# Prefix sums in two halves, unread matrix products, and key transposes ahead of the previous chunk's scores, in an attention and mixing kernel

## The chip, the core and the metric

One core of one Trainium2 chip runs the whole program. Its engines are TensorE (PE in the profile, with PEld for its weight loads), VectorE (DVE), ScalarE (ACT), GpSimd (POOL), and SyncE (SP), which here only issues transfers. The metric is device time in microseconds (us), the median of several executions.

## What is computed

The reference runs three layers on 4 batches of 768 steps, with 8 heads of 48 (384 channels).

1. A linear attention with a complex decay. At step t the state of a head decays by a complex number per row, the product of key and value is added, and the output is the query times the real part of the state:

```python
mag = np.sqrt(a_re * a_re + a_im * a_im)
scale = np.minimum(mag, 0.999) / (mag + 1e-06)
for t in range(S):
    new_re = ar * S_re - ai * S_im
    new_im = ar * S_im + ai * S_re
    S_re, S_im = (new_re + k_t v_t, new_im)
    y[t] = q_t @ S_re
```

2. A mixer: `u = x + (relu(x.T @ w_tok1) @ w_tok2).T`, then `u + relu(u @ w_ch1) @ w_ch2`.
3. A gated layer: `xk` and `xr` mix each step with the step before it; the result is `sigmoid(xr @ w_r) * (relu(xk @ w_k)**2 @ w_v)`.

## The kernel before, in words

**Attention of one batch** works on 6 chunks of 128 steps. The logarithm of the decay's magnitude and its angle are summed over time; then each query and key is turned and scaled by its sum, so that within a chunk the output is a masked product of scores with values, and across chunks a state is carried.

The setup stages have letters in the tables `SEQ0` (batch 0) and `SEQ1`: S, L, A and R make log magnitude (`X3`) and angle (`X2`) of three chunks at a time; C J sums chunk J; D makes the scale factors. A sum is a product with a triangular matrix (`tri32`) into one PSUM bank for the magnitude and one for the angle. ScalarE and VectorE take the sum out of the bank; then a product with the complementary triangle (`anti32`) completes the bank's total of the chunk, and the next chunk's triangle is added to it. So each chunk's products wait until the chunk before has been taken out (`sums`, `add`). Batches 0 and 1 do this in fp32, batches 2 and 3 with fp16 halves.

The chunk stages are in `ORD0` and `ORD1`: b turns the angles into cosine and sine (tile `cs`, line 453) and scales (line 458); w splits the value into fp16 high and low parts; q and k rotate (line 473) and take the high part (line 474); e takes the low parts (line 484); u is the state's products, v its evacuation; f0, f1 are the scores of four heads each (`sp`, line 497); m masks them (line 530) and splits off the fp16 high part (line 531); g takes the low part (line 535); h is the output's products (`y`, lines 548 and 550); i takes the output out (`xh`, `xl`, lines 559 and 560). The digit behind a stage says how many steps late it runs, so the stages of neighbouring chunks interleave in the table's order.

Queries and keys of a chunk are turned by DMA transposes, four to a chunk: high and low parts of q and k (line 441). They land in the tile `Rc`. Queries have two places, for odd and even chunks. Keys have two in batch 0 (the second is `kt`), but a single one in batches 1 to 3, so there the next chunk's keys can be transposed only when this chunk's scores have been computed.

**The dense layers** follow, in fp16 halves with three products for one. In batch 0 the first of them is accumulated chunk by chunk during the attention, in two PSUM banks `h1a` and `h1b` (line 598); their evacuation (line 627) starts the rest. The **weights** arrive in 51 pieces of 64-bit words; VectorE rebuilds fp32 from them (lines 258 to 260), ScalarE and VectorE split them into halves (lines 270 and 274), and their range is checked: a sum of squares on ScalarE (line 265), and a smallest value on VectorE (line 267, first 10 pieces) or a second pass on ScalarE (line 269, the others).

**The order.** The batches' attention and dense stages and the weight pieces are generators that are stepped by their estimated costs; the tile scheduler then places every instruction on its engine by priority (`P_EV`, `P_PE`, `P_W`; a larger offset goes earlier) and by data. Each engine runs its instructions in that fixed order. SP issues all transfers, in one fixed order too, and a transfer that must wait holds those behind it.

## Time and profile before

| | us |
|---|---|
| three runs, median | 858.17 |
| their range | 849.31 to 862.32 |
| the profiled execution | 854.39 |
| its span in the profile | 852.6 |
| the first attention (to the first dense evacuation) | 137 |

The profiled execution is one more run, 3.8 us below the median. Engines work side by side, so their busy times do not add up to the span. The trace gives each instruction's start and busy time, what its engine waited for, and the clock that TensorE was granted.

### The profile page before, as it was taken

To read this page: it belongs to the slowest core of one execution; us is meant where nothing else is said; L and a number is where in the kernel's file an instruction comes from. 1 tells how busy PE (TensorE), PEld (TensorE's weight loads), DVE (VectorE), ACT (ScalarE), POOL (GpSimd) and SP (SyncE) were. 2 spreads that over 40 slices of the span, in tenths; PEclk is the share of its full clock that TensorE was granted. 3 is DMA by queue.
4 is the path that set the end of the run, shared out by engine and by line. 5 is a ranking of instruction groups with operands and counts; after the bars stand their busy time and mean duration, and the time that the engine had idled before them with its cause. 6 is when DMAs were issued, how large, how long until landed. Compare 5 with 4: busy or idle time off the path is not lost.

```text
span 852.6 us, 14967 instructions
## 1 busy us (share of the span) xinstructions
PE 736.3 (86%) x5868; PEld 456.2 (54%) x5868; DVE 586.4 (69%) x1152; ACT 557.8 (65%) x1166; POOL 19.5 (2%) x51
## 2 busy tenths in 40 slices
PE   0636758999879978998999899999899999999996
PEld 0214544555545545555565555666565666666563
DVE  5987788999987985976767656776957434151622
ACT  7864559988789868964656769774648543142642
POOL 3000000000000000000000000000000000010000
PEclk9965658999999999999999999999999999999998
DMA  6428793445494394115230850031612420000000
GB/s 204 122 81 164 183 224 124 131 123 162 101 183 121 71 193 100 38 56 130 45 74 15 159 120 23 23 95 41 106 38 60 78 53 2 1 1 1 1 28 32
DMA packets 132941, 74.78 MB, mean 88 GB/s; under 512 B 104576, under 2 KB 126336, under 8 KB 132864
## 3 DMA queue, kind: packets, MB, share of 16 engines
q1 hardware_dynamic: 132864, 73.76, 36.3%
q8 instruction: 48, 0.79, 0.4%
q14 instruction: 29, 0.24, 0.1%
HBM read 43.85 MB, written 4.72 MB: 57 GB/s over the span
## 4 chain that ended last, share of the span: by engine, by line
PE 45%; ACT 20%; DVE 16%; DMA 14%; issue 3%; SPq 0%; ACTq 0%; DVEq 0%
PE ps L598 21%; PE a L598 15%; PE sp L497 3%; ACT X L303 3%; DMA Rc<-ql 3%; DMA Rc<-kl 2%; DMA Rc<-kh 2%; DMA X<-by_time_a_re_dram 2%; DMA CH<-in_qk_dram 2%; ACT tmp L730 1%; PE y L550 1%; ACT ps L765 1%; DMA wst<-in_moe_w_k_dram 1%; DMA wst<-in_moe_w_ch_dram 1%; ACT Rc L531 1%
## 5 line engine op out<-in xcount | busy, mean ns | idle before, releaser
L598 PEld LDWEIGHTS <-wc 128*128 128x128 f16 x1728 | 167.7, 98 | 114.1 <-issue 9.5
L598 PE MATMUL a<-g,wc 128*128 128x384 f16 x864 | 163.9, 327 | 0.0
L598 PE MATMUL ps<-uh,wc 128*128 128x384 f16 x576 | 158.1, 328 | 4.8 <-DVE g L691 3.0
L598 PE MATMUL a<-wv,g 128*128 128x384 f16 x576 | 110.7, 327 | 2.6 <-ACT g L767 2.3
L598 PE MATMUL ps<-xkh,wk 128*128 128x384 f16 x384 | 104.9, 326 | 0.5 <-DVE g L768 0.4
L690 ACT ACTIVATE g<-ps 128x384 f16<-128x384 f32 x96 | 46.5, 484 | 87.0 <-PE ps L598 86.6
L691 DVE SCALAR_TENSOR_TENSOR g<-ps,g 128x384 f16<-128x384 f32 x96 | 53.0, 553 | 73.0 <-ACT g L690 72.8
L598 PE MATMUL ps<-ul,wc 128*128 128x384 f16 x288 | 94.4, 328 | 0.0
L497 PE MATMUL sp<-Rc 96*128 96x128 f16 x504 | 62.5, 235 | 26.7 <-DMA Rc<-kh 16.2
L598 PEld LDWEIGHTS <-g 128*128 128x128 f16 x576 | 54.7, 98 | 38.0 <-ACT g L767 4.5
L598 PEld LDWEIGHTS <-wk 128*128 128x128 f16 x576 | 54.5, 97 | 33.1 <-issue 1.2
L768 DVE TENSOR_TENSOR g<-ps,g 128x384 f16<-128x384 f32 x64 | 35.4, 554 | 47.8 <-ACT g L767 47.5
L598 PE MATMUL ps<-xkl,wk 128*128 128x384 f16 x192 | 62.7, 326 | 0.0
L497 PEld LDWEIGHTS <-Rc 96*128 96x128 f16 x504 | 39.5, 105 | 35.3 <-DMA Rc<-kh 18.6
L765 ACT ACTIVATE ps<-ps 128x384 f32<-128x384 f32 x64 | 30.2, 473 | 39.6 <-PE ps L598 35.4
L548 PE MATMUL y<-CH,Rc 96*128 96x48 f16 x480 | 46.3, 191 | 8.3 <-DMA Rc<-qh 8.2
L515 PE MATMUL u<-CH,kh 128*128 128x48 f16 x320 | 39.1, 193 | 13.5 <-ACT kh L474 13.5
L550 PE MATMUL y<-CH,Rc 128*128 128x48 f16 x504 | 46.4, 190 | 4.8 <-ACT Rc L531 3.6
L473 DVE TENSOR_TENSOR Wc<-cs,X 128x768 f32<-128x768 f32 x48 | 44.9, 951 | 1.5 <-ACT cs L303 1.2
L530 DVE TENSOR_TENSOR m<-sp,tri 128x512 f32<-128x512 f32 x48 | 32.7, 684 | 17.9 <-PE sp L497 17.8
L550 PEld LDWEIGHTS <-Rc 128*128 128x128 f16 x504 | 32.3, 100 | 18.8 <-ACT Rc L531 12.1
L548 PEld LDWEIGHTS <-Rc 96*128 96x128 f16 x480 | 31.9, 102 | 16.7 <-DMA Rc<-qh 11.4
(219 smaller groups left out, 1518.7 us busy)
## 6 DMA issues: line engine op xcount, KB each, us to landing
CH<-in_qk_dram SPq DMA_DIRECT2D x24, 384.0 KB, 3.1
wst<-in_moe_w_ch_dram SPq DMA_DIRECT2D x24, 384.0 KB, 3.3
X<-by_time_a_re_dram SPq DMA_DIRECT2D x8, 576.0 KB, 4.5
X<-by_time_a_im_dram SPq DMA_DIRECT2D x8, 576.0 KB, 5.8
CH<-by_time_v_dram SPq DMA_DIRECT2D x24, 192.0 KB, 2.5
out_dram<-tmp SPq DMA_DIRECT2D x24, 192.0 KB, 1.9
wst<-in_moe_w_tok_dram SPq DMA_DIRECT2D x8, 384.0 KB, 3.4
wst<-in_moe_w_k_dram SPq DMA_DIRECT2D x8, 384.0 KB, 3.6
```

What stands on the lines that cost most here:

```text
L303: ins = ACT(out, x, fn, **k)
L473: TT(d[nm + "2"], d["cs"], bc2(hd((X3 if nm == "q" else X1)[:, J])), op=MUL)
L497: nc.tensor.matmul(out=sp[:, i], lhsT=Tr[J % 2]["k" + a_][0:96, h], rhs=Tr[J % 2]["q" + b_][0:96, h], start=n_ == 0, stop=n_ == 2)
L515: nc.tensor.matmul(out=U[:, h], lhsT=sets[J % 2]["k" + a_][:, h], rhs=d["v" + b_][:, h], start=J == 0 and h == 0 and n_ == 0, stop=h == H ...
L530: TT(m, st[J]["S", g], tri.unsqueeze(1).to_broadcast([128, 4, 128]), op=MUL)
L548: nc.tensor.matmul(out=y[:, h], lhsT=Tr[J % 2]["q" + a_][0:96, h], rhs=b_[:, h], start=n_ == 0, stop=False)
L550: nc.tensor.matmul(out=y[:, h], lhsT=M16[g][m_][:, h % 4], rhs=d[v_][:, h], start=J == 0 and n_ == 0, stop=n_ == 2)
L598: nc.tensor.matmul(out=ps, lhsT=lh[a_], rhs=rh[b_], start=start and n_ == 0, stop=stop and n_ == 2)
L690: ACT(part[:, 0], ps, ACTF.Relu)
L691: STT(part[:, 1], ps, 0.0, part[:, 0], op0=MAX, op1=SUB)
L765: ACT(ps, ps, ACTF.Relu)
L768: TT(part[:, 1], ps, part[:, 0], op=SUB)
```

## The change

It has six parts.

- **Sums of batch 0** (`products`, `add`). Angles and magnitudes of both halves are made first, and then the sums run in the order 0, 3, 1, 4, 2, 5, each half in its own two banks. The second half starts with products of chunks 0 to 2 with a matrix of equal numbers (`ones32`), so it needs no result of the first.
- **A carry instead of the complement.** From chunk to chunk within a half, and in batch 1 from each chunk to the next, ScalarE copies the last 32 rows of the bank to SBUF (`carry32`), and a product with `last32` adds the last of these rows to the next chunk's fresh bank. The products with `anti32` go in batches 0 and 1. The tile `X4` goes; its numbers are written over `X2`.
- **Unread products** (`warm`, `keep_busy`). In batch 0, products of 128x128 whose result nobody reads are put on TensorE: 50 ahead of the sums, 10 behind each sum, 20 behind each chunk stage that computes on TensorE, 750 in all. They have the lowest priority, and they write the columns 384 to 511 of the bank whose first 384 columns are `h1b`.
- **Weight checks.** The first 12 pieces lose the square sum, the smallest value and the high part's copy on ScalarE; VectorE gets a bitwise check (xor and or in one instruction) and the copy.
- **Two places for the transposed keys** in all batches (`KT`).
- **`ORD1`**: in batches 1 to 3 the stages q, k and e of a chunk, and so its transposes, come ahead of the scores of the chunk before.

```diff
-SEQ0 = "S0 L0 S1 L1 A0 R0 C0 C1 C2 D0 A1 R1 C3 C4 C5 D1 T0 T1 T2 T3 T4 T5 T6 T7"
+SEQ0 = "S0 L0 S1 L1 B1 A0 R0 A1 R1 C0 C3 C1 C4 C2 D0 C5 D1 T0 T1 T2 T3 T4 T5 T6 T7"
 ORD0 = "u1 f01 f11 b0 q0 k0 e0 i2 v1 m01 m11 g01 g11 h01 h11 w0"
-ORD1 = "b0 w0 u1 v1 f01 q0 m01 g01 h01 f11 k0 m11 g11 h11 e0 i1"
+ORD1 = "b0 u1 v1 q0 k0 e0 w0 f01 m01 g01 h01 f11 m11 g11 h11 i1"
-N_MIN = 10
+N_FILL, N_FILL0, N_WARM, P_FILL = 20, 10, 50, 2000
+N_DVE, WBITS = 12, 0x38000000
...
-    anti32 = [const.tile([128, 128], F32, name=f"anti32{i}") for i in range(2)]
+    ones32 = [const.tile([128, 128], F32, name=f"ones32{i}") for i in range(2)]
+    KT = const.tile([128, 2, H, 128], F16, name="KT")
+    last32 = const.tile([128, 128], F32, name="last32")
...
-    X4 = const.tile([128, NJ, C], F32, name="X4")
+    odd = two.tile([128, 4, C], F16, tag="hl", name="odd").rearrange("p a f -> p (a f)").bitcast(I32)[:, 0:384]
+    carry32 = [CH[:, 5:7], CH[:, 3:5]]
...
             g = t.bitcast(F32)[:, :, :, 1]
-            ACT(sq, g, ACTF.Square, accum_out=col("wide"))
-            if i < N_MIN:
-                RED(col("wmin"), g, axis=AX.XY, op=MIN, apply_absolute_value=True)
+            if i < N_DVE:
+                r = odd.rearrange("p (k n) -> p k n", k=kk)
+                STT(r, t[:, :, :, 1], WBITS, r, op0=ALU.bitwise_xor, op1=ALU.bitwise_or)
+                TS(dst[0], w, sc, None, op0=MUL)
             else:
+                ACT(sq, g, ACTF.Square, accum_out=col("wide"))
                 ACT(sq, sq, ACTF.Relu, scale=-(2.0 ** 30), bias=col_c[:, 10:11], accum_out=col("tiny"))
-            ACT(dst[0], w, ACTF.Copy, scale=sc)
...
-        def add(J, o, ps, X, later):
+        def add(J, o, ps, X):
+            k = J // 3 if b == 0 else 0
+            first = J == 3 * k
             with tc.high_priority(offset=P_PE):
                 if plain:
-                    m = (anti32 if later else tri32)[o // 2]
-                    nc.tensor.matmul(out=ps, lhsT=m, rhs=X[:, J], start=J == 0 and not later, stop=True, skip_group_check=True)
-                else:
+                    for i in range(J if first else 0):
+                        MM(out=ps, lhsT=ones32[o // 2], rhs=X[:, i], start=i == 0, stop=False)
+                    MM(out=ps, lhsT=tri32[o // 2], rhs=X[:, J], start=J == 0 or not first, stop=first)
+                    if not first:
+                        MM(out=ps, lhsT=last32[96:128], rhs=carry32[k][96:128, o // 2], start=False, stop=True)
+                    if J + 1 < NJ and J + 1 != 3 * k + (3 if b == 0 else NJ):
+                        ACT(carry32[k][96:128, o // 2], ps[96:128], ACTF.Copy)
+                    return
+                if J > 0:
                     for i in range(2):
-                        nc.tensor.matmul(out=ps, lhsT=anti if later else tri, rhs=hl[J][:, o + i], start=J == 0 and not later and i == 0,
-                                         stop=True, skip_group_check=True)
+                        nc.tensor.matmul(out=ps, lhsT=anti, rhs=hl[J - 1][:, o + i], start=False, stop=True, skip_group_check=True)
+                for i in range(2):
+                    nc.tensor.matmul(out=ps, lhsT=tri, rhs=hl[J][:, o + i], start=J == 0 and i == 0, stop=True, skip_group_check=True)
...
+        both = ((X3, 0), (X2, 2))
+        def products(J):
+            k = J // 3 if b == 0 else 0
+            if J == 0 or plain:
+                for o, tag in ((0, "u"), (2, "y")):
+                    acc[J, o] = bank(tag, k if at[0] is None else at[0], [128, C])
+            else:
...
+            for X, o in both:
+                last_mm.clear()
+                add(J, o, acc[J, o], X)
+                if b == 0:
+                    keep_busy(N_FILL0)
         def sums(J):
-            if J == 0:
-                for o, tag in ((0, "u"), (2, "y")):
-                    acc[o] = bank(tag, 1, [128, C])
-                parts(0)
-            parts(J + 1)
+            if J == 0 or b > 0 or J % 3:
+                products(J)
+            if b == 0 and J == 0:
+                products(3)
             if J % 3 == 0:
-                rest[J // 3] = wide()
-            both = ((X3, 0), (X2, 2))
-            for X, o in both:
-                add(J, o, acc[o], X, False)
+                rest[J // 3] = wide() if b > 0 or J == 0 else R[:, 1024:1024 + 3 * C].rearrange("p (j f) -> p j f", j=3)
             yield 0.4 if plain else 1.3
-            ACT(X1[:, J], acc[0], ACTF.Copy, bias=ROUND_L)
+            ps = [acc.pop((J, o)) if plain else acc[J, o] for o in (0, 2)]
+            ACT(X1[:, J], ps[0], ACTF.Copy, bias=ROUND_L)
             r = tmp2()
-            ACT(r, acc[2], ACTF.Copy, bias=ROUND)
-            STT(rest[J // 3][:, J % 3], X1[:, J], ROUND_L, acc[0], op0=SUB, op1=SUB)
-            STT(X4[:, J], r, ROUND, acc[2], op0=SUB, op1=SUB)
-            if J < NJ - 1:
-                for X, o in both:
-                    add(J, o, acc[o], X, True)
+            ACT(r, ps[1], ACTF.Copy, bias=ROUND)
+            STT(rest[J // 3][:, J % 3], X1[:, J], ROUND_L, ps[0], op0=SUB, op1=SUB)
+            STT(X2[:, J], r, ROUND, ps[1], op0=SUB, op1=SUB)
             yield 1.2
+        last_mm = []
+        def MM(**k):
+            last_mm[:] = [nc.tensor.matmul(**k)]
+        def keep_busy(n):
+            with tc.high_priority(offset=-P_FILL):
+                for _ in range(n):
+                    ins = nc.tensor.matmul(out=h1_ps[1][:, C:512], lhsT=tri, rhs=tri, start=False, stop=False, skip_group_check=True)
+                    behind([ins], last_mm)
+        def warm(k):
+            t = one.tile([128, 128], F16, tag="warm", name="warm")
+            ACT(t, X3[:, 3 * k, 0:128], ACTF.Copy)
+            for _ in range(N_WARM):
+                nc.tensor.matmul(out=h1_ps[1][:, C:512], lhsT=tri, rhs=t, start=False, stop=False, skip_group_check=True)
+            yield 0.0
...
         Tr = [{"qh": Trs[2 * i], "ql": Trs[2 * i + 1], "kh": Trs[4], "kl": Trs[5]} for i in range(2)]
+        Tr[1]["kh"], Tr[1]["kl"] = KT[:, 0], KT[:, 1]
         if b == 0:
-            kt = one.tile([128, 2, H, 128], F16, tag="rl", name="kt")
-            Tr[1]["kh"], Tr[1]["kl"] = kt[:, 0], kt[:, 1]
             M16 = [M16[0], [one.tile([128, 4, 128], F16, tag=f"h1{s}", name=f"M1{s}") for s in "hl"]]
...
@@ -581,14 +638,21 @@
             for stage, back in order:
                 if 0 <= s - back < NJ:
-                    yield stage(s - back)
+                    last_mm.clear()
+                    cost = stage(s - back)
+                    if b == 0 and last_mm:
+                        keep_busy(N_FILL)
+                    yield cost
...
         load(0, "qv")
-        kinds = {"S": squares, "L": logs, "A": slopes, "R": angles, "C": sums, "D": decays, "T": step}
+        if b == 0:
+            h1_ps.extend((ps_a.tile([128, C], F32, tag="a2", name="h1a"), ps_1.tile([128, 512], F32, tag="s", name="h1b")))
+            nc.tensor.matmul(out=h1_ps[1], lhsT=tri, rhs=qk16["qh"][:, 0:4], start=True, stop=True)
```

The `...` in the diff leaves out, among other lines, the counterpart of the check at the end and the new constant `last32`, and that the products of the stages f, h and u are issued through `MM`, which only remembers the last of them.

Three places show what the scheduler makes of it. The first is TensorE at the end of the first attention. `h1a` and `h1b` are the two banks of the first dense product, `xh`, `xl` its input, `wt` weights, and `ps` a bank of the second dense product, which reads `h1h`. Before:

```order
L598 MATMUL h1a<-xh,wt_102 128x384
L598 LDWEIGHTS wt_101
L598 MATMUL h1b<-xl,wt_101 128x384
L598 LDWEIGHTS wt_102
L598 MATMUL h1b<-xh,wt_102 128x384
L598 LDWEIGHTS h1h
L598 MATMUL ps<-wt_103,h1h 128x384
```

With the change (`h1b<-tri` is an unread product; 24 of them stand between the last `h1a` product and the first of the last nine `h1b` products, and 80 and 40 more between those nine, which come in threes, one three for each of the last three chunks):

```order
L662 MATMUL h1a<-xh,wt_104 128x384
L451 LDWEIGHTS tri
L451 MATMUL h1b<-tri 128x128
...
L662 LDWEIGHTS h1h
L662 MATMUL ps<-wt_105,h1h 128x384
...
L662 MATMUL h1b<-xh,wt_103 128x384
L662 LDWEIGHTS wt_103
L662 MATMUL h1b<-xl,wt_103 128x384
L662 LDWEIGHTS wt_104
L662 MATMUL h1b<-xh,wt_104 128x384
```

The products of `h1b` of the last chunks moved behind 144 unread products, which stand between the last `h1a` product and them.

The second is ScalarE at the same place: `h1h<-h1a` and `h1h<-h1b` are the two evacuations, `X` and `wide` belong to the setup of batch 1, `wc` and `wst` to the weights. Before:

```order
L325 ACTIVATE wide<-X_121 128x1152
L627 ACTIVATE h1h<-h1a 128x384
L627 ACTIVATE h1h<-h1b 128x384
L182 ACTIVATE seen,stat_low<-h1h 128x96
L270 ACTIVATE wc_107<-wst 128x384
L269 ACTIVATE wc_108,stat_tiny<-wc_108,col_c 128x384
L303 ACT_TABLE_LOAD
L303 ACTIVATE X_120<-X_120 128x1152
L646 ACTIVATE uh<-ps 128x384 x2
```

With the change:

```order
L691 ACTIVATE h1h<-h1a 128x384
L283 ACTIVATE wc_109<-wst 128x384
L190 ACTIVATE seen,stat_low<-h1h 128x96
L282 ACTIVATE wc_110,stat_tiny<-wc_110,col_c 128x384
L319 ACT_TABLE_LOAD
L319 ACTIVATE X_124<-X_124 128x1152 x2
L283 ACTIVATE wc_107<-wst 128x3x128
L281 ACTIVATE wc_108,stat_wide<-wst 128x3x128
L319 ACTIVATE X_122<-X_122 128x1152
...
L283 ACTIVATE wc_107<-wst 128x3x128
L691 ACTIVATE h1h<-h1b 128x384
```

The two evacuations stood side by side; now 14 instructions, weight steps and setup stages of batch 1 that stood behind both, lie between them.

The third is SP in batch 1, the transposes of its first chunks (`kh`, `kl`, `qh`, `ql`; `CH<-by_time_v_dram` is the next value chunk). Before:

```order
L441 DMA_TRANSPOSE Rc<-kh 128x8x128
L441 DMA_TRANSPOSE Rc<-ql 128x8x128
L441 DMA_TRANSPOSE Rc<-kl 128x8x128
L441 DMA_TRANSPOSE Rc<-qh 128x8x128
L435 DMA CH<-by_time_v_dram 128x384
```

With the change:

```order
L500 DMA_TRANSPOSE Rc<-kh 128x8x128
L500 DMA_TRANSPOSE Rc<-ql 128x8x128
L500 DMA_TRANSPOSE Rc<-kl 128x8x128
L494 DMA CH<-by_time_v_dram 128x384
L500 DMA_TRANSPOSE KT<-kh 128x8x128
```

The second chunk's high keys go to `KT`, a place of their own, and stand directly behind the value load; they no longer share `Rc` with the first chunk's.

## Rows read from the trace of the kernel before

**Rows 1.** the page: span, share of TensorE, and the granted clock in 40 slices

```profile
span 852.6 us, 14967 instructions
PE 736.3 (86%) x5868; PEld 456.2 (54%) x5868; DVE 586.4 (69%) x1152; ACT 557.8 (65%) x1166; POOL 19.5 (2%) x51
PEclk9965658999999999999999999999999999999998
```

**Rows 2.** five stretches: bounds and length, busy time by engine, PEclk, DMA

```profile
17.11:58.65 41.54, 21.15 (x44) 9.87 (x44) 38.24 (x85) 31.71 (x65) 0.00 (x0) 0.87 0.32 95
58.65:135.92 77.27, 46.60 (x580) 35.98 (x581) 62.66 (x110) 45.78 (x96) 0.00 (x0) 0.61 0.80 185
137.20:170.00 32.80, 29.08 (x162) 16.41 (x163) 31.23 (x68) 32.48 (x72) 0.00 (x0) 0.91 0.36 109
170.00:225.00 55.00, 54.73 (x293) 31.33 (x292) 53.69 (x130) 45.42 (x120) 2.99 (x7) 1.00 0.40 122
225.00:335.00 110.00, 92.20 (x911) 57.63 (x909) 91.00 (x184) 90.55 (x197) 0.74 (x2) 0.95 0.67 143
```

**Rows 3.** DVE waits (total, times, longest) and ScalarE's rows, 17.11 to 58.65

```profile
DVE wide L395 <- ACT X L391: 2.8, 2, 1.4
48.53 0.49 ACT L391 ACTIVATE X<-u 128x384 f32<-128x384 f32 x1 [1.39 <-PE u L371]
```

**Rows 4.** timeline (start, busy) of VectorE where the first chunk begins

```profile
58.38 0.35 DVE L258 TENSOR_SCALAR wf<-wst 128x384 int32<-128x384 int32 x1
58.65 0.35 DVE L453 TENSOR_SCALAR cs<-X 128x384 int32<-128x384 int32 x1
58.92 0.55 DVE L259 SCALAR_TENSOR_TENSOR wf<-wst,wf 128x384 int32<-128x384 int32 x1
59.39 0.61 DVE L458 SCALAR_TENSOR_TENSOR X<-CH,col_c,X 128x384 f32<-128x384 f32 x1
```

**Rows 5.** VectorE's waits, 57 to 140: total, times, longest

```profile
DVE m L530 <- PE sp L497: 3.9, 2, 2.5
DVE xl L560 <- ACT xh L559: 3.8, 2, 2.1
DVE kl L484 <- ACT kh L474: 2.5, 2, 2.3
```

**Rows 6.** timeline: scores at either clock, and products queued behind them

```profile
70.33 2.32 PE L497 MATMUL sp<-Rc 96*128 96x128 f16 x20 [0.90 <-DMA Rc<-kl]
294.68 0.83 PE L497 MATMUL sp<-Rc 96*128 96x128 f16 x12
75.18 0.68 DVE L535 TENSOR_TENSOR M1l<-m,M1h 128x512 f16<-128x512 f32 x1
77.54 0.72 PE L497 MATMUL sp<-Rc,kt 96*128 96x128 f16 x5 [0.23 <-DMA kt<-kl]
78.05 0.25 PE L550 MATMUL y<-CH,M1l 128*128 128x48 f16 x1
```

**Rows 7.** timeline where the first attention ends

```profile
135.39 0.61 DVE L560 SCALAR_TENSOR_TENSOR xl<-y,col_c,xh 128x384 f16<-128x384 f32 x1
137.24 0.49 ACT L627 ACTIVATE h1h<-h1b 128x384 f16<-128x384 f32 x1
141.40 0.47 ACT L646 ACTIVATE uh<-ps 128x384 f16<-128x384 f32 x1
```

**Rows 8.** 225 to 720: scores, idle before; 225 to 440: waits (total, times, longest)

```profile
L497 PE MATMUL sp<-Rc 96*128 96x128 f16 x432 | 52.8, 223 | 20.5 <-DMA Rc<-kh 12.9 <-DMA Rc<-ql 3.7 <-DMA Rc<-kl 1.9
PE sp L497 <- DMA Rc<-kh: 10.0, 5, 3.2
```

**Rows 9.** timeline of the key transposes of one chunk, and the scores after them

```profile
308.83 1.40 SPq L441 DMA_TRANSPOSE Rc<-kh  x1
310.33 2.90 SPq L441 DMA_TRANSPOSE Rc<-kl  x1
315.22 0.28 PE L497 MATMUL sp<-Rc 96*128 96x128 f16 x2 [3.17 <-DMA Rc<-kh]
```

More of the change, by code (lines that the diff above doesn't have):

```diff
@@ L62 @@
 ROUND_L = 1.5 * 2.0 ** (11 + L_S + 1)
-STATS = {"wp": 8, "wm": 8, "wide": 51, "tiny": 51 - N_MIN, "wmin": N_MIN, "wsum": 51, "xsum": 48, "osum": 24, "low": 36, "re": 8}
+STATS = {"wp": 8, "wm": 8, "wide": 51 - N_DVE, "tiny": 51 - N_DVE, "wbits": 1, "wsum": 51, "xsum": 48, "osum": 24, "low": 36, "re": 8}
 NSTAT = sum(STATS.values()) + STATS["wp"] + STATS["wm"]
@@ L193, in setup_small @@
         t = tmps.tile([128, 512], F32, tag="tmp", name="tri32")
-        nc.sync.dma_start(out=t[:, 0:256], in_=c_tri)
+        nc.sync.dma_start(out=t[:, 0:384], in_=c_tri)
         nc.gpsimd.tensor_copy(tri, t[:, 0:128])
@@ L198, in setup_small @@
             ACT(tri32[i], t[:, 0:128], ACTF.Copy, scale=sc)
-            ACT(anti32[i], t[:, 128:256], ACTF.Copy, scale=sc)
+            nc.gpsimd.memset(ones32[i], sc)
+        ACT(last32, t[:, 256:384], ACTF.Copy)
+        nc.gpsimd.memset(odd, 0)
         nc.gpsimd.memset(ones, UNIT)
@@ new lines, in attention @@
+        both = ((X3, 0), (X2, 2))
[5 more added lines that the diff above has]
+            else:
+                for o in (0, 2):
+                    acc[J, o] = acc[J - 1, o]
+            if not plain:
+                if J == 0:
+                    parts(0)
+                parts(J + 1)
+            for X, o in both:
[3 more added lines that the diff above has]
+                    keep_busy(N_FILL0)
@@ L547, in s_h @@
                         for n_, (a_, b_) in enumerate((("h", th), ("h", tl), ("l", th))):
-                            nc.tensor.matmul(out=y[:, h], lhsT=Tr[J % 2]["q" + a_][0:96, h], rhs=b_[:, h], start=n_ == 0, stop=False)
+                            MM(out=y[:, h], lhsT=Tr[J % 2]["q" + a_][0:96, h], rhs=b_[:, h], start=n_ == 0, stop=False)
                     for n_, (m_, v_) in enumerate(((0, "vh"), (0, "vl"), (1, "vh"))):
-                        nc.tensor.matmul(out=y[:, h], lhsT=M16[g][m_][:, h % 4], rhs=d[v_][:, h], start=J == 0 and n_ == 0, stop=n_ == 2)
+                        MM(out=y[:, h], lhsT=M16[g][m_][:, h % 4], rhs=d[v_][:, h], start=J == 0 and n_ == 0, stop=n_ == 2)
             return 0.0
@@ L590, in attention @@
         load(0, "qv")
-        kinds = {"S": squares, "L": logs, "A": slopes, "R": angles, "C": sums, "D": decays, "T": step}
+        if b == 0:
+            h1_ps.extend((ps_a.tile([128, C], F32, tag="a2", name="h1a"), ps_1.tile([128, 512], F32, tag="s", name="h1b")))
+            nc.tensor.matmul(out=h1_ps[1], lhsT=tri, rhs=qk16["qh"][:, 0:4], start=True, stop=True)
+        kinds = {"S": squares, "L": logs, "A": slopes, "R": angles, "C": sums, "D": decays, "T": step, "B": warm}
         for word in (SEQ0 if b == 0 else SEQ1).split():
```

22 lines of the change are left out of this document (12 added, 10 removed).

## The prediction

> **What bounds the kernel now.** I read the page first: a span of 852.6, TensorE busy for 86% of it, and the row of granted clock, whose slices 3 to 6 (43 to 128 us) stand at 5 to 6 tenths while later ones stand at 9 [rows 1]. So most of the run is TensorE at nearly full speed, and what differs is the first 137 us. Cut into stretches [rows 2], the setup's sums (17.11 to 58.65) are VectorE's: busy 38.24 of 41.54. The chunk phase (58.65 to 135.92) has no engine full: VectorE 62.66, TensorE 46.60 and ScalarE 45.78 of 77.27, with a mean clock of 0.61, that is 78% of the time at the lower of the two levels (1.2 and 2.4 GHz; 1.0 - 0.78 x 0.5 = 0.61). It is a chain that passes from engine to engine. From 170 on, in the dense layers, TensorE is busy 54.73 of 55.00. Where batches 1 to 3 run their attention beside the dense layers, it has gaps again: 92.20 of 110.00 in 225 to 335, at 0.95. Next came the waits: whom VectorE waits for in the first attention [rows 3, 5], and what TensorE waits for in the later ones [rows 8]. A change can gain in three places: the setup, the chunk phase, and those gaps.
>
> The profiled execution took 854.4, 3.8 less than the median of the runs shown, 858.2. I sum against 854.4 and carry the sum to 858.2.
>
> **Sums side by side, carry and weight checks, up to the first chunk.** VectorE's idle time before the first chunk is 41.54 - 38.24 = 3.3, and 2.8 of it are its two waits for the copy of a sum [rows 2, 3]. That is all that side by side sums can take away here, since VectorE has other work beside the rest. Against it stands new work on VectorE. From start to start a shift-and-mask on a weight piece takes 0.27, a two-operand integer step 0.47 [rows 4]. Of the 12 high-part copies that come to VectorE, 10 fall before the first chunk: 10 x 0.27 = 2.7; by the new order two residuals of values move behind it (2 x 0.55, the busy time of such a row [rows 4], = 1.1 less), and one bitwise check more than there were smallest-value checks stands there, 0.47. So about 2.1 more. Sum: -2.8 + 2.1, rounded to **-0.8** with the rest of the idle time; ends -3.3 + 2.1 = -1.2, and +2.1 if VectorE then waits elsewhere. ScalarE loses its checks, which hang on nothing here: busy 31.71 of 41.54 [rows 2], so 0.
>
> **The chunk phase with the unread products.** 20 of a chunk's 24 score products take 2.32 at the low clock, 0.116 each; 12 take 0.83 at the full one, 0.069 with the tail of the last in it [rows 6]. The dense stretch gives a price without such tails: 54.73 / 293 = 0.187 for 384 columns [rows 2], 0.062 for 128. I take 0.066 for a score. On the chain lie about 20 per chunk (the four behind them overlap the mask), so the full clock brings 20 x (0.116 - 0.066) = 1.0 per chunk, 6.0 in six chunks. I count the scores alone: the state's and output's products have slack of a step in the table. VectorE has 2.1 more to do here as well (2 copies, the two residuals, the end of the check). Sum **-3.9**. Ends: 0 + 2.1 = +2.1 if the clock doesn't matter; at most the three longest sums of waits go, 3.9 + 3.8 + 2.5 = 10.2 [rows 5], so -8.1. What the unread products themselves cost: 436 of them stand among the chunk stages; at 0.062 they take 27, at 0.116 they take 51. TensorE's idle time there is 77.27 - 46.60 = 30.7 [rows 2], so at the full clock they fit, and their cover is that idle time; faster products of its own add to it.
>
> They run in order, though: lowest priority only means a late place. At 77.54 the last five scores of a chunk start, and a product `y` whose input `M1l` was there at 75.86 (75.18 + 0.68) runs at 78.05, behind them [rows 6]: what stands in front is waited for, whether it is read or not. The Trainium skill's page "TensorE: Matmul & The Clock Gate" (Part 2, the step on LDWEIGHTS) states the same as a rule against this change: products stay in program order, and only weight loads are pulled ahead. The trace agrees, with the 78.05 against 75.86; what the rule would make of 20 unread products that stand before each stage's next product is the third rival.
>
> **The end of the first attention.** Of `h1b`, the products of the last three chunks stand behind 144 unread ones, and the evacuation of `h1b` behind 14 ScalarE instructions. Before, `xl` of the last chunk is taken at 135.39, `h1b` is evacuated at 137.24, and the second dense product's first result at 141.40 [rows 7]. 144 x 0.062 = 8.9 more. Part comes back: in 137.20 to 170.00 TensorE has 32.80 - 29.08 = 3.7 idle and runs at 0.91, which is about 1.5 lost to the low clock [rows 2]. So 8.9 - 5.2 = **+3.7**. Ends: 0, if the unread products fill time in which TensorE waits for the last chunk anyway; 144 x 0.116 = +16.7 at the low clock. ScalarE's moved work is not lost: it is busy 32.48 of 32.80 there, and does earlier what it did later.
>
> **Carry in batch 1.** Ten copies on ScalarE, 0.49 each as the copy of a sum [rows 3], 4.9 in all; in 170 to 225, where they fall, ScalarE has 55.00 - 45.42 = 9.6 idle while TensorE is full [rows 2]. **0**; ends 0 and +4.9. The `anti32` products that go are TensorE's, few, and replaced by others.
>
> **Keys in two places and the new `ORD1`.** In batches 1 to 3 the 432 scores have 20.5 idle before them, 12.9 put down to the high keys, 3.7 to the low queries, 1.9 to the low keys [rows 8]. In one chunk: the high keys' transpose takes SP 1.40 from 308.83, the low keys' 2.90 from 310.33, and the scores wait 3.17 for the first and start at 315.22 [rows 9]. With one place the transpose cannot start until the chunk before has been scored; with two places and q, k, e ahead of the scores, it can be issued some stages earlier. On SP the load of the next values now stands ahead of the second chunk's first key transpose, and that load waits for the stage w, which comes after e: its copy and residual, about 0.49 and 0.55 by like rows [rows 3, 4], can hold the transposes behind by some 1.0, which the earlier place covers; if it doesn't, the lower end takes it in. TensorE is the fullest engine there, so its idle time counts. I take the 12.9 and leave the queries' and the low keys' waits, since SP still issues the four one after the other. Ends: 0 (another wait comes) and -18.5 (all). With fewer gaps the low-clock part of 225 to 335 (0.05 x 2 x 110 = 11 us at half speed, up to 5.5 lost) shrinks; most gaps stay, so -1.5. **-14.4**.
>
> **Sum**: -0.8 - 3.9 + 3.7 + 0 - 14.4 = -15.4: 839.0 on the profiled execution, 842.8 on the median. Two per cent, about what a measurement of this kernel can tell from no change, is 841.0 or 875.3.
>
> **The cases.**
>
> *As summed*, 832 to 850, chance 0.40, half of it under 841.0. For it: the largest term is a wait that the profile names by transfer.
>
> *Rival 1: full clock throughout the first attention, and all transposes in time.* Then the terms are -0.8, -8.1, 0 at the junction (unread products in idle time), -18.5 - 1.5: -28.9, or 829 on the median. For it: the later dense stretch, with TensorE busy 54.73 of 55.00, has a clock of 1.00, and the chunk phase, with 60% busy, 0.61 [rows 2]. Against it: VectorE is busy 62.66 of 77.27 there. Chance 0.24. The same page (Part 1, on the clock gate) has a rule for it: the clock is released under sustained work and falls back after idle stretches; the two stretches agree, and by that rule the time is this rival's 829.
>
> *Rival 2: another wait takes the transposes' place.* In 225 to 335 VectorE is busy 91.00 and ScalarE 90.55 of 110.00 [rows 2], and the chunk stages pass through both; moving q, k and e ahead delays the masks of the chunk before. If a third of the 12.9 is left: -0.8 - 3.9 + 3.7 - 4.3 = -5.3, or 853. Chance 0.18.
>
> *Rival 3, slower: the unread products are in the way.* If the clock stays low, 436 x 0.116 = 51 in the chunk phase against 30.7 idle, +19.9; the junction 16.7 - 3.7 = +13.0; the setup -0.8; batches 1 to 3 -14.4: +17.7, or 876; without the batches' gain 890; with the price between the two clocks, 860 and up. It decides from 30.7 / 436 = 0.070 per product on. It is also the case in which the change does not raise the clock. For it: every unread product must be passed in order, and at 0.062 only 3.7 of idle time are left over. Against it: with them TensorE has hardly a pause. Chance 0.16, of which 0.12 over 875.3.
>
> The last 0.02 is for anything else. So **842.8**; 8 in 10 need 822 to 868 (left out are most of rival 3 and the lowest of rival 1). Faster by over 2%: 0.20 + 0.24 + 0.01 = 0.45; within: 0.20 + 0.18 + 0.04 + 0.01 = 0.43; slower: 0.12.
>
> **What would show it.** The first `cs` of chunk 0 near 58; clock digits of 9 in slices 3 to 6; in the chunk phase, scores of 12 products in 0.8 and VectorE's wait for `sp` under 1; between the two `h1h` evacuations a gap of 8 to 12; in batches 1 to 3 the scores' waits for transposes at 6 or less, and the `KT` transposes issued before the chunk before has been scored. The prediction is wrong if the chunk phase takes over 80 us (rival 3), if it takes under 70 (rival 1), or if TensorE's idle time in the later attentions keeps its size under other names (rival 2).

## The result: 0.7% slower

The changed kernel takes 861.88 us (median of 20 runs, 858.78 to 866.43) against 856.22 (849.31 to 862.32): a ratio of 1.0072, 95% interval 1.0055 to 1.0090. I had forecast 842.8, in 822 to 868 at 8 in 10; the time lies inside that range, but the direction was forecast the wrong way. By my 2% bound it is "no change", to which I gave 0.43; by this finer measurement the change costs 6 us instead of bringing 15.

The page of the changed kernel, with the lines that answer to [rows 1]:

```profile
span 860.4 us, 16500 instructions
PE 768.3 (89%) x6627; PEld 489.1 (57%) x6627; DVE 592.2 (69%) x1168; ACT 553.9 (64%) x1143; POOL 19.6 (2%) x54
PEclk9987989899999999999998999999999999999999
```

The clock rose: slices 3 to 6 went from 6, 5, 6, 5 to 8, 7, 9, 8. TensorE is 32.0 longer busy, and the time did not fall. The stretches that answer to [rows 2] (bounds and length, busy time of PE, PEld, DVE, ACT, POOL, PEclk, DMA share, GB/s):

```profile
17.11:59.24 42.13, 30.49 (x222) 19.46 (x221) 40.53 (x94) 26.62 (x43) 0.00 (x0) 0.98 0.28 85
59.24:137.00 77.76, 57.10 (x994) 51.27 (x995) 63.71 (x112) 42.54 (x87) 0.00 (x0) 0.86 0.83 189
137.00:170.00 33.00, 29.25 (x272) 20.27 (x271) 29.56 (x60) 30.85 (x64) 0.00 (x0) 0.90 0.29 91
170.00:225.00 55.00, 53.31 (x269) 28.00 (x268) 51.50 (x122) 50.41 (x129) 1.75 (x6) 1.00 0.44 134
225.00:335.00 110.00, 95.53 (x929) 59.99 (x928) 97.61 (x204) 91.75 (x206) 0.75 (x3) 0.98 0.60 143
```

The first chunk begins at 59.24, 0.6 later than before. The chunk phase has a clock of 0.86 in place of 0.61 and is no shorter: the last output of batch 0 leaves PSUM at 136.51, before at 134.48. From there to the last output of batch 3 it is 577.8 against 571.9, and from that to the end 146 in both. The distance to the kernel before is 2.0 at the last outputs of batches 0 and 1, and 7.1 and 8.0 at those of batches 2 and 3: most of it opens in batch 2. VectorE's waits in the chunk phase (total, times, longest), which answer to [rows 5]:

```profile
DVE Wc L532 <- ACT cs L319: 3.4, 1, 3.4
DVE m L589 <- PE sp L445: 3.1, 2, 2.3
DVE xl L619 <- ACT xh L618: 3.0, 2, 1.5
DVE kl L543 <- ACT kh L533: 0.2, 1, 0.2
```

The wait for scores fell by 0.8 only, and what the `kl` wait lost, a wait for ScalarE's cosine (`cs`, 0.9 before) took. The 2.3 that is left of the wait for scores stands behind the first chunk's, and those still ran at the low clock, as did most of the fifth chunk's. Twenty scores of the first, third and fifth chunk (timeline, against [rows 6]):

```profile
71.84 2.34 PE L445 MATMUL sp<-Rc 96*128 96x128 f16 x20
89.77 1.29 PE L445 MATMUL sp<-Rc 96*128 96x128 f16 x20 [1.62 <-DMA Rc<-kl]
116.81 2.31 PE L445 MATMUL sp<-Rc 96*128 96x128 f16 x20 [1.92 <-DMA Rc<-kl]
```

From 59 to 69, ahead of the first scores, TensorE is busy 1.96 of 10 and the granted clock is 0.50: the unread products do not keep it up everywhere. In batches 1 to 3, the scores in 225 to 720 with the idle time before them, and TensorE's longest waits there, against [rows 8]:

```profile
L445 PE MATMUL sp<-Rc 96*128 96x128 f16 x216 | 26.3, 222 | 6.7 <-DVE m L589 4.4 <-DMA Rc<-kl 2.3
L445 PE MATMUL sp<-Rc,KT 96*128 96x128 f16 x216 | 24.9, 222 | 0.8 <-DMA KT<-kl 0.8
```

```profile
PE a L662 <- ACT g L831: 5.0, 3, 3.0
PE sp L445 <- DVE m L589: 4.4, 4, 2.5
PE y L445 <- DVE xl L619: 3.1, 3, 1.8
PE ps L662 <- DVE g L755: 2.8, 4, 1.9
```

Transposes are hardly waited for any longer: 18.5 became 3.1. In their place stand waits for VectorE and ScalarE. The order moved the transposes ahead of the masks, and now the scores wait for the bank that a late mask still holds (`m`), the outputs for `xl`, the dense layers for `g`.

The end of the first attention (timeline; the second evacuation answers to [rows 7]):

```profile
138.81 0.47 ACT L691 ACTIVATE h1h<-h1a 128x384 f16<-128x384 f32 x1
141.64 4.63 PE L451 MATMUL h1b<-tri 128*128 128x128 f16 x80
149.16 0.33 PE L662 MATMUL h1b<-xh,wt 128*128 128x384 f16 x1
151.15 0.48 ACT L691 ACTIVATE h1h<-h1b 128x384 f16<-128x384 f32 x1
151.69 0.82 PE L662 MATMUL ps<-wt,h1h 128*128 128x384 f16 x4 [2.20 <-ACT h1h L691]
```

`h1b` is evacuated at 151.15, 13.9 later than before. The unread products look like the reason; experiment 3 shows that they are not.

### The profile page after: what moved, and what is told of

Same layout as the page of the kernel before. It is cut to its first block, busy times and chain, and to the rows that moved or that the text cites. A ratio compares the mean times of both kernels' runs of the same rounds, so it can differ in the third digit from the quotient of the medians.

```text
span 860.4 us, 16500 instructions
## 1 busy us (share of the span) xinstructions
PE 768.3 (89%) x6627; PEld 489.1 (57%) x6627; DVE 592.2 (69%) x1168; ACT 553.9 (64%) x1143; POOL 19.6 (2%) x54
## 4 chain that ended last, share of the span: by engine, by line
PE 42%; ACT 20%; DVE 20%; DMA 12%; issue 5%; SPq 1%; ACTq 0%; DVEq 0%
PE ps L662 20%; PE a L662 13%; PE y L445 3%; ACT X L319 3%; DMA X<-by_time_a_re_dram 2%; PE sp L445 2%; PE u L445 2%; DMA wst<-in_moe_w_ch_dram 2%; DVE g L755 2%; DVE Wc L532 1%; DMA Rc<-ql 1%; DMA CH<-in_qk_dram 1%; DMA Rc<-kl 1%; DVE kl L543 1%; ACT ps L830 1%
## 5 line engine op out<-in xcount | busy, mean ns | idle before, releaser
L445 PEld LDWEIGHTS <-Rc 96*128 96x128 f16 (+1 forms) x1272 | 62.8, 99 | 48.1 <-ACT Rc L590 12.1
L445 PE MATMUL y<-CH,Rc 96*128 96x48 f16 (+1 forms) x984 | 56.4, 184 | 11.0 <-DMA Rc<-qh 3.4
L445 PE MATMUL u<-CH,kh 128*128 128x48 f16 x320 | 36.5, 187 | 16.4 <-ACT kh L533 15.9
L451 PE MATMUL h1b<-tri 128*128 128x128 f16 x700 | 50.2, 225 | 0.0
L451 PEld LDWEIGHTS <-tri 128*128 128x128 f16 x700 | 43.9, 101 | 7.8 <-issue 5.5
L445 PE MATMUL sp<-Rc 96*128 96x128 f16 x288 | 34.3, 236 | 13.4 <-DMA Rc<-kl 5.8
L590 ACT ACTIVATE Rc<-m 128x512 f16<-128x512 f32 x42 | 26.2, 624 | 28.7 <-DVE m L589 22.8
L319 ACT ACTIVATE X<-X,col_c 128x1152 f32<-128x1152 f32 x32 | 40.1, 1253 | 3.2 <-DVE X L355 1.6
```

What stands on the lines that cost most here:

```text
L319: ins = ACT(out, x, fn, **k)
L445: last_mm[:] = [nc.tensor.matmul(**k)]
L451: ins = nc.tensor.matmul(out=h1_ps[1][:, C:512], lhsT=tri, rhs=tri, start=False, stop=False, skip_group_check=True)
L590: ACT(M16[g][0], m, ACTF.Copy)
```

## The experiments

Each ratio is to the kernel before, run on the same chip beside it (median 854 to 856), with its 95% interval; prices in us are worked out from the ratios. "Last output" is the time at which ScalarE takes the last output of batch 0 out (134.48 before, 136.51 changed).

### The unread products

**1. None of them.** From the changed kernel:

```diff
-N_FILL, N_FILL0, N_WARM, P_FILL = 20, 10, 50, 2000
+N_FILL, N_FILL0, N_WARM, P_FILL = 0, 0, 0, 2000
...
-SEQ0 = "S0 L0 S1 L1 B1 A0 R0 A1 R1 C0 C3 C1 C4 C2 D0 C5 D1 T0 T1 T2 T3 T4 T5 T6 T7"
+SEQ0 = "S0 L0 S1 L1 A0 R0 A1 R1 C0 C3 C1 C4 C2 D0 C5 D1 T0 T1 T2 T3 T4 T5 T6 T7"
```

> The changed kernel with none of the 750 unread products. Theory J (the junction): the change loses its time where the last products of h1b, and through them its evacuation and the first dense layer, stand behind 144 unread products (first dense product on uh at 163.9 against 152.1 before, +11.8), and the low clock that the unread products remove costs the chunk phase next to nothing, because that phase is a chain through VectorE and ScalarE. J expects the junction's 11 to 12 back, a chunk phase of 75 to 79 at a clock near 0.6 and about 851 (848 to 854). Rival C (the clock is worth what I predicted, 6 or more, and something of the same size hides it): the chunk phase grows to over 82 and the time is 857 or more. Rival S (the lag after the first attention comes from the setup of batch 1 on ScalarE, not from the unread products): the lag stays, 860 or more.

860.13, ratio 1.0070 (1.0047 to 1.0094). Last output 136.1. The two `h1h` evacuations stood side by side again (138.1 and 138.5), and it gained nothing: theory J fell. Rival C's number came, its reason didn't (the chunk phase takes 78.1 for 77.3, not over 82). Theory S's number came too, here and in experiment 2; experiments 12 and 16 look at the setup of batch 1.

**2. None in the last steps.** From the changed kernel:

```diff
-                    if b == 0 and last_mm:
+                    if b == 0 and last_mm and s < 5:
```

> The changed kernel without the unread products of the steps from the fifth on (180 fewer; 570 stay, and by the new order none stands between the last h1a and the last h1b product). Theory J: the h1b evacuation is back beside that of h1a, within 1; the first dense product on uh comes at 151 to 154; total 851 (848 to 854), equal to the kernel with no unread product at all within 3. Rival C: better than that kernel by 4 or more, since the clock of the first four chunks is kept. Rival S: 859 or more.

860.67, 1.0065 (1.0037 to 1.0094). `h1b` evacuated at 139.97. J fell here too.

Both runs left out instructions, and the scheduler then ordered everything behind them anew. So I fixed the order: experiments 3 and 5 chain every instruction of each engine to the order of another kernel and leave out its unread products alone.

**3. The changed kernel's order without its 750 unread products.**

```diff
-N_FILL, N_FILL0, N_WARM, P_FILL = 20, 10, 50, 2000
+N_FILL, N_FILL0, N_WARM, P_FILL = 0, 0, 0, 2000
...
+        behind([LOG[k_]], [LOG[last_]])
```

> The changed kernel with exactly its order of all other instructions on every engine, but without its 750 unread products. Theory T (in this order they only take TensorE's time: 144 x 0.062 = 8.9 at the end of the first attention, before the evacuation of h1b, and nothing else): 853 to 859. Theory C (what they cost there they bring back by the clock): 861 to 866. Theory S (the evacuation of h1b, which stands behind 14 instructions of ScalarE, ends the wait there anyway, so the unread products cost nothing): 860 to 863, with h1b evacuated at 150 as before.

860.58, 1.0055 (1.0032 to 1.0078): theory S. Its timeline:

```profile
143.24 0.53 PE L114 MATMUL h1b<-xh,wt 128*128 128x384 f16 x1
151.80 1.46 PE L114 MATMUL ps<-wt,h1h 128*128 128x384 f16 x4 [8.03 <-ACT h1h L114]
```

The last product of `h1b` is 5.9 earlier, and TensorE then waits 8.03 for the evacuation, which ScalarE makes at 151.27, after its 14 other instructions. The unread tail costs nothing by itself; with it in the program the scheduler puts ScalarE's work in front, without it (2) it does not. The stretch 0 to 135 of this kernel, and then of the changed one (columns as above):

```profile
0.00:135.00 135.00, 66.45 (x584) 43.65 (x585) 109.33 (x209) 78.79 (x136) 8.65 (x18) 0.73 0.64 164
```

```profile
0.00:135.00 135.00, 86.20 (x1160) 68.93 (x1161) 109.19 (x209) 78.55 (x136) 8.66 (x18) 0.91 0.66 165
```

A clock of 0.73 or 0.91, and the last output at 136.89 or 136.51: in this order the clock is worth 0.4 there. Of it 0.3 is there at the first chunk (59.50 or 59.24); the chunk phase is 0.1 shorter.

**4. Side by side sums with 570 unread products, none in the last steps**, on the kernel before with experiment 15's sums:

```diff
...
+                    if b == 0 and last_mm and s < 5:
+                        keep_busy(N_FILL)
...
```

> The kernel with the sums of batch 0 side by side (847) and 570 unread products beside them and beside the first chunks, none behind the last h1a product. It keeps TensorE's clock up in the first attention and nothing else. If the chunk phase is a chain through VectorE and ScalarE that the clock doesn't shorten: 845 to 850, with the last x evacuation of batch 0 within 1 of 132.1. If the clock is worth the 6 that I predicted and the tail at the end of the first attention had hidden it: 841 or less.

840.24, 0.9841 (0.9802 to 0.9880): the fastest of all, against 0.9933 without the unread products. Yet its last output is at 132.15, where that kernel has 132.08. The gain stands behind the first attention, where nothing is unread. So the time is that of the expectation's second case, and the last output that of its first.

**5. The order of experiment 4 without its unread products**, by the chain of experiment 3:

```diff
-N_FILL, N_FILL0, N_WARM, P_FILL = 20, 10, 50, 2000
+N_FILL, N_FILL0, N_WARM, P_FILL = 0, 0, 0, 2000
...
+        behind([LOG[k_]], [LOG[last_]])
```

> The kernel with side by side sums and 570 unread products (840), with exactly its order of all other instructions on every engine, but without the unread products. Theory O (they act through the order that the scheduler gives the rest): 838 to 843. Theory C (they act through the clock): 846 or more, as the side by side kernel without them (847).

848.75, 0.9915 (0.9888 to 0.9942). Stretch 0 to 135 of this kernel, and of experiment 4:

```profile
0.00:135.00 135.00, 69.62 (x632) 45.67 (x633) 107.49 (x200) 94.96 (x186) 8.29 (x17) 0.70 0.65 168
```

```profile
0.00:135.00 135.00, 89.28 (x1210) 69.77 (x1211) 109.26 (x202) 96.87 (x190) 8.29 (x17) 0.94 0.67 168
```

Here the clock counts: last output 134.21 against 132.15, so 2.1 in the first attention. Of that 1.5 is there at the first chunk (57.16 against 55.64), after the setup's sums; the chunk phase itself, with the scores of five of its six chunks at full clock against none, is 0.5 shorter. The distance grows to 7.6 by the last output of batch 1 without a further difference in the work. Theory O fell. Why the distance grows there is open. In the changed kernel's order the same kind of products brings nothing (3); that an order suits the clock it was made with is a guess.

**6 and 7. 18 or 22 unread products a stage for 20**, otherwise experiment 4:

```diff
-N_FILL, N_FILL0, N_WARM, P_FILL = 20, 10, 50, 2000
+N_FILL, N_FILL0, N_WARM, P_FILL = 18, 10, 50, 2000
```

> The kernel with side by side sums and unread products (840), with 18 unread products per stage in place of 20: some 50 fewer of 570, 3 us of TensorE time in its idle stretches, and another order of the setup and attention of batch 1. If prices belong to the parts: 838 to 842. If the order behind them decides: off by 4 or more, 844 to 855.

> The same with 22 unread products per stage. If prices belong to the parts: 838 to 842. If the order decides: off by 4 or more, to either side.

845.22, 0.9896 (0.9857 to 0.9935), and 847.15, 0.9909 (0.9880 to 0.9938). Nearly the same work and nearly the same last output (131.94 and 132.84), 5 and 7 slower; with 22, `h1b` is evacuated 4.6 later (139.05 for 134.48). So the order that comes out behind a part is worth up to 7, as much as most prices here, and the 840, the best of three such orders, may be in part luck.

### Keys and stage order

**8. One place for the keys and the old order**, from the changed kernel:

```diff
-ORD1 = "b0 u1 v1 q0 k0 e0 w0 f01 m01 g01 h01 f11 m11 g11 h11 i1"
+ORD1 = "b0 w0 u1 v1 f01 q0 m01 g01 h01 f11 k0 m11 g11 h11 e0 i1"
...
-        Tr[1]["kh"], Tr[1]["kl"] = KT[:, 0], KT[:, 1]
+        if b == 0:
+            Tr[1]["kh"], Tr[1]["kl"] = KT[:, 0], KT[:, 1]
```

> The changed kernel with the transposed keys of batches 1 to 3 in one place again and the old stage order of these batches; everything else, the unread products too, as changed. If the keys and the order brought the 14 that I predicted, this loses them: 876. By the lag of the dense products in the two traces (it falls from 12 to 21 just after the first attention to 9 to 11 from the middle of batch 1 on) they brought 3 to 9: 865 to 871. If another wait took the transposes' place altogether: 861 to 863.

864.83, 1.0130 (1.0102 to 1.0157): loses 5 by the ratios, 3 by the times.

**9. Two places, old order**, from the changed kernel:

```diff
-ORD1 = "b0 u1 v1 q0 k0 e0 w0 f01 m01 g01 h01 f11 m11 g11 h11 i1"
+ORD1 = "b0 w0 u1 v1 f01 q0 m01 g01 h01 f11 k0 m11 g11 h11 e0 i1"
```

> The changed kernel with two places for the keys but the old stage order in batches 1 to 3. If the place alone is what helps: as the changed kernel, 860 to 864. If only the place and the order together help: as with one place. If the new order delays the masks of the chunk before and so eats what the place brings: faster than the changed kernel by 3 or more, 859 or less.

861.48, 1.0085 (1.0058 to 1.0111): not told apart from the changed kernel. Against experiment 8 the place alone brings 3 to 4 here: the scores' waits for transposes in 225 to 720 fall from 13.2 to 7.3. The new order adds nothing that these runs can tell.

**10. Two places alone**, on the kernel before:

```diff
...
+        Tr[1]["kh"], Tr[1]["kl"] = KT[:, 0], KT[:, 1]
...
```

> The kernel before with two places for the transposed keys in all batches and nothing else (to make room, the angle sums of chunk J are written over the angle input of chunk J-1 instead of into a tile of their own; the order of all instructions is otherwise as before). One place instead of two cost the changed kernel 3 to 5, so the place alone should bring 3 to 6: 849 to 852. If the idle time moves to other waits, as the changed kernel's trace shows for TensorE (20.5 before scores fell, the idle time in 137 to 820 did not): 854 to 856. My predicted term alone (-14.4) would be 841.

855.72, 1.0009 (0.9981 to 1.0037). Its scores in 225 to 720:

```profile
L500 PE MATMUL sp<-Rc 96*128 96x128 f16 x216 | 26.9, 219 | 6.3 <-DMA Rc<-kh 3.1 <-DMA Rc<-ql 1.3 <-DVE m L533 1.0
L500 PE MATMUL sp<-Rc,KT 96*128 96x128 f16 x216 | 25.6, 231 | 9.6 <-DMA KT<-kh 6.0 <-DMA Rc<-ql 2.0 <-DMA KT<-kl 1.2
```

The chunks with a place of their own still wait 6.0 for it. The stages that make the keys come late in the old order, so on this kernel a free place alone brings nothing; on the changed kernel (9) it did.

**11. Two places and the new order**, on the kernel before:

```diff
-ORD1 = "b0 w0 u1 v1 f01 q0 m01 g01 h01 f11 k0 m11 g11 h11 e0 i1"
+ORD1 = "b0 u1 v1 q0 k0 e0 w0 f01 m01 g01 h01 f11 m11 g11 h11 i1"
...
+        Tr[1]["kh"], Tr[1]["kl"] = KT[:, 0], KT[:, 1]
...
```

> The kernel before with two places for the keys and the new stage order, and nothing else. The place alone did nothing (13.6 of the 18.5 of the scores' waits for transposes stayed). If the order makes the place useful, the scores' waits for transposes fall below 6, and the time is 850 to 852 by what the changed kernel lost without both, 841 by my prediction. If the stages that the order delays (masks, outputs) take the time back: 854 to 857.

850.26, 0.9953 (0.9928 to 0.9979): -4, not -14.4. Its longest waits in 225 to 720:

```profile
PE sp L500 <- DVE m L533: 5.4, 6, 2.2
PE ps L601 <- DVE g L694: 5.1, 2, 3.2
PE a L601 <- ACT g L770: 4.3, 3, 2.4
```

The scores' waits for transposes are 9.0 there, of 18.5 before: half the exchange of the changed kernel, without its other parts, and not below the 6 that I expected. TensorE's idle time between the last outputs of batches 0 and 3 is 41.7 here, and was 40.7 before.

### VectorE's checks, the carry, the sums

**12. The weight checks alone**, on the kernel before:

```diff
...
-            ACT(sq, g, ACTF.Square, accum_out=col("wide"))
-            if i < N_MIN:
-                RED(col("wmin"), g, axis=AX.XY, op=MIN, apply_absolute_value=True)
+            if i < N_DVE:
+                STT(r, t[:, :, :, 1], WBITS, r, op0=ALU.bitwise_xor, op1=ALU.bitwise_or)
+                TS(dst[0], w, sc, None, op0=MUL)
...
```

> The kernel before with the weight checks and high-part copies of the first 12 pieces moved to VectorE and nothing else. Theory K (the carry through ScalarE in batch 1 is what costs): 853 to 857, no change. Rival W (VectorE is the full engine up to the first chunk, so the 2 us it gets there and the 2 in the chunk phase count, and they move the setup of batch 1 later as well): 859 or more.

859.77, 1.0079 (1.0058 to 1.0099): rival W. Up to 134.5, this kernel and the one before:

```profile
0.00:134.50 134.50, 64.47 (x587) 43.56 (x588) 110.02 (x210) 76.30 (x131) 8.36 (x16) 0.73 0.65 165
```

```profile
0.00:134.50 134.50, 67.26 (x622) 45.66 (x623) 106.10 (x198) 88.54 (x173) 8.01 (x15) 0.73 0.66 168
```

ScalarE gets 12.2 free and VectorE 3.9 more. The first chunk is not late (57.17, before 58.65), and the last output only 1.1; but the first VectorE instruction of batch 1's setup (the smallest `a_re`) runs at 142.0, before at 136.4. TensorE's idle time between the last outputs of batches 0 and 3 is 45.0, before 40.7.

**13. The smallest-value checks moved the other way**, to ScalarE (`N_MIN = 0`), on the kernel before, and **14.** on experiment 4:

```diff
-N_MIN = 10
+N_MIN = 0
...
```

> The kernel before with the smallest-value check of the first 10 weight pieces moved from VectorE to ScalarE's second pass, as the other pieces have it: the opposite of moving checks to VectorE. If VectorE's work before and in the first attention counts in full at the end (the checks put some 4 there and cost 6.7), taking about 4 from it brings 3 to 7: 848 to 852. If ScalarE, which gets 10 passes more, is as much in the way: 855 to 860.

> The kernel with side by side sums and 570 unread products (840), with the smallest-value checks of 10 weight pieces on ScalarE instead of VectorE. Alone that did -1. If VectorE's work in the first attention counts at the end: 833 to 838. If ScalarE is as full: 839 to 845.

852.82, 0.9989 (0.9963 to 1.0015), and 843.42, 0.9863 (0.9834 to 0.9892): no gain. On 14 the last output even comes at 138.2 for 132.15. That fits a ScalarE that is by then as full as VectorE; it was not shown apart.

**15. Side by side sums in batch 0 alone**, on the kernel before:

```diff
-SEQ0 = "S0 L0 S1 L1 A0 R0 C0 C1 C2 D0 A1 R1 C3 C4 C5 D1 T0 T1 T2 T3 T4 T5 T6 T7"
+SEQ0 = "S0 L0 S1 L1 A0 R0 A1 R1 C0 C3 C1 C4 C2 D0 C5 D1 T0 T1 T2 T3 T4 T5 T6 T7"
...
```

> The kernel before with the sums of batch 0 alone in two halves side by side, with the carry within a half, and nothing unread. My term for the setup was -2.8 (the two waits of VectorE), so 852; theory K says the first attention hides it: 853 to 857; if setting up both halves first delays the first chunk: 857 to 860.

847.34, 0.9933 (0.9910 to 0.9955): faster, below all three expectations. Its first chunk, and the longest of VectorE's waits in 17.1 to 56, where the longest had been 2.8 [rows 3]:

```profile
56.29 0.35 DVE L495 TENSOR_SCALAR cs<-X 128x384 int32<-128x384 int32 x1
```

```profile
DVE X L416 <- ACT t L413: 0.5, 1, 0.5
```

The first chunk and the last output come 2.4 earlier; the rest of the 5.7 comes behind the first attention. (The angle sums of batches 1 to 3 are placed as in experiment 10.)

**16. The carry in batch 1 alone**, on the kernel before:

```diff
...
+                if b == 1:
+                    nc.tensor.matmul(out=ps, lhsT=tri32[o // 2], rhs=X[:, J], start=True, stop=J == 0)
+                    if J > 0:
+                        nc.tensor.matmul(out=ps, lhsT=last32[96:128], rhs=carry32[0][96:128, o // 2], start=False, stop=True)
...
```

> The kernel before with the sums of batch 1 alone by the carry (fresh bank, last rows copied by ScalarE, product with the last row) in place of the complement. Theory K: the 12 sums of batch 1, which took 26.5 from first to last evacuation and 29 to 32 in the changed kernels, get longer, the setup of batch 1 ends 5 to 10 later, and its attention with it: 861 to 866. My prediction's value (4.9 of ScalarE work in its idle time): 855. If the delay of that setup comes from elsewhere: 853 to 857.

859.54, 1.0054 (1.0036 to 1.0073): slower, as theory K has it, by less than its 861 to 866. First and last magnitude sum of batch 1 that ScalarE takes out, and the last of the scale factors:

```profile
166.94 0.49 ACT L401 ACTIVATE X<-u 128x384 f32<-128x384 f32 x1
201.16 0.49 ACT L401 ACTIVATE X<-u 128x384 f32<-128x384 f32 x1 [0.17 <-PE u L376]
208.57 1.35 DVE L417 SCALAR_TENSOR_TENSOR X<-wide,X 128x1152 f32<-128x1152 f32 x1
```

34.2 from first to last, before 26.5 (165.22 to 191.76); the scale factors end 10.8 later (197.77 before). The copies are short, but each stands in a queue of other ScalarE work, and now the next chunk's sum waits behind it. The last output of batch 1 is only 1.2 later (339.00 for 337.76); that of batch 2 is 5.2 later (521.06 for 515.86). TensorE's idle time between the last outputs of batches 0 and 3 is 45.3, before 40.7.

### Putting together what paid

**17. Side by side, keys and order** (the edits of 15 and 11), and **18.** the same with 570 unread products (and that of 4):

```diff
-ORD1 = "b0 w0 u1 v1 f01 q0 m01 g01 h01 f11 k0 m11 g11 h11 e0 i1"
+ORD1 = "b0 u1 v1 q0 k0 e0 w0 f01 m01 g01 h01 f11 m11 g11 h11 i1"
...
+        Tr[1]["kh"], Tr[1]["kl"] = KT[:, 0], KT[:, 1]
...
```

> The kernel before with the sums of batch 0 side by side (847 alone), two places for the transposed keys and the new stage order of batches 1 to 3: the changed kernel without the unread products, the weight checks on VectorE and the carry in batch 1. If the parts add up and keys with order bring the 3 to 5 that the changed kernel lost without them: 842 to 845. If what they shorten is given back to other waits: 846 to 849.

> The kernel with side by side sums and 570 unread products (840), with two places for the keys and the new stage order of batches 1 to 3 (-4 alone). If the parts add: 835 to 838. If keys and order only change the order of the rest, as good or bad luck: 838 to 848.

846.43, 0.9910 (0.9880 to 0.9940): 2 better than 15 alone, within its interval. 853.80, 0.9979 (0.9952 to 1.0006): 12 worse than experiment 4. What brings 4 on one kernel costs 12 on another. Experiment 4 stays the best: faster than both kernels, also with 18 or 22 products.

## Why the prediction was wrong, step by step

- **Sums side by side: right in mechanism, and in size where I measured it.** I said -2.8 for VectorE's two waits; alone the first chunk comes 2.4 earlier (15). In the changed kernel it comes 0.6 later, and VectorE is busy 40.53 up to there against 38.24, which is about the +2.1 that I had for the checks. That the checks ate the gain is still not shown: alone they don't delay the first chunk (12).
- **The clock, -6.0: failed.** I priced the scores by their difference at the two clocks, put 20 per chunk on the chain and took the full clock for all six chunks. Four of the six ran at it; at a fixed order the chunk phase was 0.1 shorter for that (3), and 0.5 in experiment 4's order, where five did (5). My count of what lies on the chain was wrong: in [rows 5] VectorE waits for scores only twice in six chunks, 3.9 in all, and I took 6.0. By windows, the time at the low level in 0 to 135 fell by 2 x (0.91 - 0.73) x 135 = 49 in the changed order and by 2 x (0.94 - 0.70) x 135 = 65 in the other. The Trainium skill's page "TensorE: Matmul & The Clock Gate" (section "HAM oscillation") prices such time at half its length, which would be, as an estimate, 24 and 32. The runs show 0.4 and 2.1 at the last output (8.5 of the whole time in the second), and the measurement decides: in the first of these stretches VectorE was busy 109.19 of 135 and TensorE 86.20.
- **Unread products in the way (rival 3): did not happen.** They fitted TensorE's idle time: between the first cosine and the last output it is 31.2 without them (3) and 20.7 with them.
- **The junction, +3.7: the wait came, by another engine.** `h1b` is evacuated 13.9 later, but without the tail it would be too (3): the ScalarE order that I showed and set to "not lost" ends the wait. I had weighed the order of TensorE's queue alone. The Trainium skill's page "TensorE: Matmul & The Clock Gate" (section "Architectural detail") states strict order for ScalarE and VectorE, and the 8.03 of experiment 3 agrees. What it costs at the end was not measured apart; taking the tail away and ordering anew gained nothing (2). The 1.5 that I took back here for the low clock is also half of what my way of reckoning in 225 to 335 gives (0.09 x 32.80 = 3.0).
- **VectorE's checks, +4.2 in two terms: right that they count, and they count for more**, 6.7 alone (12). I let the chunk phase's 2.1 be paid for by the clock, and for a setup of batch 1 that starts 5.6 later I had no term.
- **The carry, 0 (0 to +4.9): failed, at its upper end.** 4.6 alone (16). I asked whether ScalarE had 4.9 idle in the stretch; the question was who waits for each copy.
- **Keys and order, -14.4: the step that failed most.** I let TensorE's idle time count in full because TensorE is the fullest engine there. In the changed kernel the waits went as forecast (18.5 to 3.1), the time did not: keys and order brought 4 alone (11, waits 9.0), and 5 were lost when they were taken out of the changed kernel (8). That is the mechanism of rival 2, to which I gave 0.18: masks, `xl` and `g` late instead. Its sign came as I had put it: between the last outputs of batches 0 and 3 TensorE's idle time, 40.7 before, is 41.7 with keys and order alone (11) and 40.1 in the changed order without unread products (3); in the changed kernel it is 34.0, with unread products in it. VectorE 91.00 and ScalarE 90.55 of 110.00 in [rows 2] had pointed there, and VectorE is at 97.61 now. Rival 2's 853 did not come: checks and carry cost 11.3 one by one, where I had put 4.2.

Together: side by side -0.67%, keys with order -0.47%, checks +0.79%, carry +0.54%, unread products nothing in this order: +0.2%, measured +0.7%. A second route agrees in the main: experiment 17 is the changed kernel without unread products, checks and carry, at 0.9910, and experiment 1 is it without unread products alone, at 1.0070. So checks and carry together cost 1.6% where they stand, against 1.33% one by one; in this step are also smaller differences that no run prices apart, such as the place of the `anti` products of batches 2 and 3. The missing half per cent is of the size that experiments 6 and 7 move by order alone, and so are the single prices of checks and carry. Which waits in batches 1 and 2 make it up is open; and so is why keys with order cost 12 on experiment 4.

## What to carry to other kernels

A wait that the profile names by its releaser is worth its length only if nothing else is nearly as late. Look at the busy share of the engines that the same work passes through next. Price a small instruction that is put into a chain by who stands behind it, not by the idle time of its engine. Where a scheduler orders everything, fix the order before pricing a part; here a change of two idle products a stage moved the whole by 5 to 7 us.

## What the runs showed of the hardware

A ScalarE copy of 32 rows out of PSUM takes as long as one of 128. In the kernel of experiment 16, the carry's copy and the copy of a whole sum:

```profile
159.52 0.48 ACT L378 ACTIVATE CH<-u 32x384 f32<-32x384 f32 x1
```

It is 0.48, against 0.49 for the 128 rows of the first sum shown there. So the carry's ten copies cost ScalarE what ten whole evacuations would.
